# Sink-window attention woven with a cosine FFN: q and k of the third half loaded in 32-row groups and turned by VectorE, and four tiles for the sinks' rows of v

## The chip, the cores and the metric

The kernel runs on one core of one Trainium2 chip. The time is device microseconds, the median of three runs. The engines are TensorE (PE in the profile; its weight loads are PEld), VectorE (DVE), ScalarE (ACT), GpSimd (POOL) and SyncE (SP), which issues the transfers of this case.

## The reference

Three layers follow each other. Attention has 4 batches, 8 heads, 768 positions and head dimension 64; a position sees the 4 sinks and the 128 positions that end with itself. Its output, 3072 tokens by 512, goes through an FFN with a cosine, and that through a mixture of 8 experts, of which each token takes one.

```python
scores = scale * np.matmul(q, k.transpose(0, 1, 3, 2))
keep = is_sink | in_window
a = softmax(np.where(keep, scores, -1e9))
x = np.matmul(a, v)              # to 3072 x 512
h = x @ w_in                     # 512 -> 2048
x = (h * np.cos(h)) @ w_out      # 2048 -> 512
logits = x @ w_gate + modality_bias[modality_id]
e = argmax(logits)
out = softmax(logits)[e] * (relu(x @ w1[e]) @ w2[e])
```

## The kernel before

**Halves and pairs.** Attention is cut into eight halves, `hb` 0 to 7: a half is 384 positions (three blocks of 128) of one batch, for all eight heads. Heads are taken two at a time, so a half has four pairs (`pr` 0 to 3), with one head in partitions 0 to 63 and the other in 64 to 127. The third half, which the change touches, is `hb = 2`: the first 384 positions of the second batch, with three blocks of keys. It runs from about 113 to 204 us in the trace. For each pair, `attn_front` loads q and k (and starts v), brings them to the form [head dimension, position] in `qT` and `kT`, and hands on to `mid` (scores `ps`, row maxima, exponentials into `Pb`) and `rest` (division, transposes `pt`, product with v in `po`).

**Two ways to turn q and k.** Up to the third half (`hb < STACK = 3`) lines 442 and 443 load 128 positions on the partitions, in runs of 64 numbers; TensorE transposes block by block into a PSUM bank (`pq` at L466, `pk` at L480, three blocks each in the third half), and ScalarE copies the bank to `qT` (L472) and `kT` (L494). From the fourth half on, lines 437 and 439 load four groups of 32 partitions, one for each half of each head's dimension, in runs of 32 numbers, so that VectorE's transposes of 32x32 blocks (L462, L476) give the wanted form by themselves. There the operands are also split in a high and a low part (`q_r` to two tiles `qT`, `k_r` to two tiles `kT`), by ScalarE (L469, L489) and VectorE (L149).

**The sinks' rows of v.** Line 451 loads the sinks' rows of v of a pair into one of two tiles, `vs_n0` and `vs_n1`, by `pr % 2`. From the fourth half on, GpSimd makes the operand `vs_r` of them (L609, L610, L149).

**The FFN.** `ffn_tile_gen` goes over 384 tokens at a time, in 16 chunks of 128 hidden columns. A chunk has 12 matmuls into a bank `hp` (two such banks); VectorE (L143, L146), ScalarE (L738) and VectorE (L149) make `ch` = h cos h of it and free the bank; ScalarE and GpSimd split it into `g_h` and `g_l` (L748, L149); and 9 matmuls `y` (L676) multiply it by the high and low part of w_out. The low part, `wo_l`, is read back from memory for each chunk (L721, three buffers). Beside the first halves a converter makes all high and low weights: loads `cv_in` and `cv_out`, chains on VectorE and ScalarE (`cv_a`, `wi_l`, `wo_l`, L301, L141, L146), and stores of `wo_l` (L304). Its last step lies at about 204 us, where the fourth half begins.

**What sets the order.** The code is written with generators that `weave` and `merge` advance by weights, and a scheduler in the framework orders the instructions of each engine. What runs is a fixed order for each engine. SP issues these transfers one after the other, and one that waits for a buffer holds up those behind it.

## Time and profile before

| | us |
|---|---|
| median of three runs | 1129.12 |
| lowest and highest | 1128.71 and 1129.29 |
| profiled execution | 1130.26 |
| its span, first to last instruction | 1128.5 |
| TensorE busy in the span | 1085.8 (96%) |
| VectorE busy in the span | 700.3 (62%) |
| mean granted clock of TensorE | 0.993 |

The span is what the views show; 1.76 us of the profiled execution lie outside it. Matmuls are pipelined, so a matmul's own duration is longer than the distance to the start of the next one; that distance is what it costs TensorE.

### The profile page before, as it was taken

The page shows a single profiled execution, that of the slowest core. Times are in us where ns is not written, and L with a number is a line of the kernel's source. Part 1 is how long each engine was busy: PE and PEld are TensorE (multiplying, and loading weights), DVE is VectorE, ACT ScalarE, POOL GpSimd, SP SyncE. Part 2 cuts the span into 40 slices and gives each one's busy share as a digit, 9 for nine tenths or more (in the row PEclk, how much of TensorE's full clock was granted, in tenths as well). Part 3 has the DMA queues.
Part 4 walks back from the last instruction along what each step waited for, and adds up shares of the span by engine and source line. Part 5 has one row for each costly group of instructions (what it writes and reads, how often), then busy time and mean ns, then how long its engine had stood idle before and what let it go on. Part 6 is the DMA issues. An engine that isn't in the chain of part 4 may idle for free.

```text
span 1128.5 us, 20688 instructions
## 1 busy us (share of the span) xinstructions
PE 1085.8 (96%) x6432; PEld 917.2 (81%) x6432; DVE 700.3 (62%) x2186; ACT 607.9 (54%) x1243; POOL 247.3 (22%) x337
## 2 busy tenths in 40 slices
PE   5989999999999999999999999999999998999995
PEld 3667777788788888888888889899889997899984
DVE  6677888777977877886787674746731225522210
ACT  4879888665676666665766553334222225422221
POOL 1232233322212221222222211321112211221110
PEclk9989999999999999999999999999999999999998
DMA  6466675433332542433342132624151115111110
GB/s 152 134 187 181 199 232 147 102 83 83 89 91 68 111 89 65 101 75 82 74 107 68 56 114 73 254 64 114 47 188 58 58 40 188 39 59 40 40 41 24
DMA packets 171155, 113.38 MB, mean 100 GB/s; under 512 B 130799, under 2 KB 138991, under 8 KB 170992
## 3 DMA queue, kind: packets, MB, share of 16 engines
q1 hardware_dynamic: 166672, 97.88, 32.3%
q0 software_dynamic: 4320, 13.65, 3.7%
q8 instruction: 63, 1.03, 0.4%
q14 instruction: 100, 0.82, 0.2%
HBM read 151.06 MB, written 19.67 MB: 151 GB/s over the span
## 4 chain that ended last, share of the span: by engine, by line
PE 82%; DVE 6%; DMA 4%; ACT 3%; issue 2%; POOL 1%; SPq 0%; DVEq 0%; ACTq 0%; POOLq 0%
PE hp L137 21%; PE y L676 20%; PE m_y L137 11%; PE m_h L137 10%; PE ps L137 5%; PE po L137 5%; DMA out_dram<-m_ot,m_ids 3%; PE pl L804 1%; PE pt L589 1%; PE mh L137 1%; PE yT L793 1%; PE m_a L1143 1%; DMA cv_in<-in_moe_w_in_dram 1%; PE pt L588 1%; PE pz L626 1%
## 5 line engine op out<-in xcount | busy, mean ns | idle before, releaser
L149 POOL TENSOR_TENSOR g_l<-ch,g_h 128x384 fp32r<-128x384 f32 x128 | 133.6, 1044 | 471.6 <-ACT g_h L748 408.6
L137 PE MATMUL hp<-xT_h,wi_h 128*128 128x384 f32 x512 | 186.4, 364 | 2.2 <-DVE ch L149 2.2
L137 PE MATMUL hp<-xT_h,wi_l 128*128 128x384 f32 x512 | 175.1, 342 | 0.0
L137 PE MATMUL hp<-xT_l,wi_h 128*128 128x384 f32 x512 | 174.5, 341 | 0.0
L676 PE MATMUL y<-wo_l,g_h 128*128 128x512 f32 x384 | 155.7, 406 | 2.2 <-DMA wo_l<-wl_scr 2.2
L676 PE MATMUL y<-wo,g_h 128*128 128x512 f32 x384 | 156.9, 410 | 0.0
L676 PE MATMUL y<-wo,g_l 128*128 128x512 f32 x384 | 154.5, 402 | 0.2 <-POOL g_l L149 0.2
L738 ACT ACTIVATE ch<-ch,cols 128x384 f32<-128x384 f32 x128 | 78.7, 616 | 107.8 <-DVE ch L146 107.1
L137 PE MATMUL m_y<-wi_h,hT 128*128 128x512 f32 x416 | 132.5, 393 | 0.7 <-issue 0.5
L146 DVE SCALAR_TENSOR_TENSOR hT<-m_h,hT 128x256 fp32r<-128x256 f32 x88 | 37.4, 424 | 151.0 <-ACTq L1337 102.3
L137 PEld LDWEIGHTS hp<-xT_h,wi_h 128*128 128x128 f32 x512 | 96.9, 189 | 15.5 <-issue 4.5
L748 ACT ACTIVATE g_h<-ch 128x384 fp32r<-128x384 f32 x128 | 66.3, 520 | 69.7 <-DVE ch L149 46.2
L137 PEld LDWEIGHTS hp<-xT_l,wi_h 128*128 128x128 f32 x512 | 97.2, 190 | 4.4 <-issue 1.0
L143 DVE TENSOR_SCALAR ch<-hp 128x384 int32<-128x384 f32 x128 | 70.8, 553 | 46.6 <-PE hp L137 35.4
L137 PEld LDWEIGHTS hp<-xT_h,wi_l 128*128 128x128 f32 x512 | 96.8, 189 | 1.7 <-issue 1.4
L137 PEld LDWEIGHTS m_y<-wi_h,hT 128*128 128x128 f32 x416 | 78.1, 188 | 17.0 <-issue 0.9
L149 DVE TENSOR_TENSOR ch<-ch,hp 128x384 f32<-128x384 f32 x128 | 70.0, 547 | 29.7 <-ACT ch L738 29.2
L551 ACT ACTIVATE Pb<-Pb,mx 128x272 f32<-128x272 f32 (+1 forms) x168 | 82.8, 494 | 8.4 <-DVE mx L534 7.5
L676 PEld LDWEIGHTS y<-wo,g_l 128*128 128x128 f32 x384 | 72.3, 188 | 15.1 <-POOL g_l L149 1.0
L676 PEld LDWEIGHTS y<-wo,g_h 128*128 128x128 f32 x384 | 72.3, 188 | 13.9 <-issue 3.6
L676 PEld LDWEIGHTS y<-wo_l,g_h 128*128 128x128 f32 x384 | 72.5, 189 | 11.3 <-DMA wo_l<-wl_scr 2.5
L1154 ACT ACTIVATE hT<-m_h 128x256 fp32r<-128x256 f32 x88 | 34.0, 387 | 87.6 <-PE m_h L137 86.6
(289 smaller groups left out, 2288.8 us busy)
## 6 DMA issues: line engine op xcount, KB each, us to landing
rw<-in_moe_w_dram SPq DMA_DIRECT2D x112, 512.0 KB
wo_l<-wl_scr SPq DMA_DIRECT2D x122, 256.0 KB
cv_in<-in_moe_w_in_dram SPq DMA_DIRECT2D x16, 512.0 KB
cv_out<-in_moe_w_out_dram SPq DMA_DIRECT2D x16, 512.0 KB
y_scr<-yt SPq DMA_DIRECT2D x24, 256.5 KB
xT_h<-xg_h SPq DMA_DIRECT2D x32, 192.0 KB
xT_l<-xg_l SPq DMA_DIRECT2D x32, 192.0 KB
wl_scr<-wo_l SPq DMA_DIRECT2D x16, 256.0 KB
```

Source lines behind the costliest of these rows:

```text
L137: PE.matmul(o, l, r, start=start, stop=stop)
L143: e.tensor_scalar(out=o, in0=i, scalar1=s1, scalar2=s2, op0=op0, op1=op1)
L146: e.scalar_tensor_tensor(out=o, in0=i0, scalar=s, in1=i1, op0=op0, op1=op1)
L149: e.tensor_tensor(out=o, in0=a, in1=b, op=op)
L551: ACT.activation(out=Pb[t][j][:, c0:c1], in_=Pb[t][j][:, c0:c1], func=AF.Exp, scale=-1.0, bias=mx[:, i:i + 1], accum_out=sm[:, i:i + 1])
L588: PE.transpose(pt[:, j, 0:P], Pb[t][j][:, 0:P], ident)
L589: PE.transpose(pt[:, j, P:2 * P], Pb[t][j][:, SEG:W3], ident)
L626: PE.transpose(pz[0:nr, t * P:(t + 1) * P], pi_, ident)
L676: i = PE.matmul(o, l, r, start=start, stop=stop)
L738: ACT.activation(out=ch, in_=ch, func=AF.Sin, scale=TWO_PI, bias=half_pi)
L748: ACT.activation(out=gh, in_=ch, func=AF.Copy)
L1154: ACT.activation(out=hT_h[f], in_=hp, func=AF.Relu)
```

## The change

For `hb = 2` the four pairs load q and k as the later halves do, in four groups of 32 partitions, and VectorE's transposes write `qT[0]` and `kT[0]` directly: this half is not split in high and low parts, so no `q_r` or `k_r` is needed. Twenty-four transposes on TensorE (12 `pq`, 12 `pk`) and eight copies on ScalarE (four at L472, four at L494) are no longer there; eight transposes on VectorE and sixteen more loads are. The eight PSUM banks of `pq` and `pk` are no longer taken. The small copies of the sinks' keys (L486, L496) read `kT[0]` in place of the bank.

From the fourth half on, the sinks' rows of v go to a tile for each pair: two more tiles, in the memory that the converter has given back, cleared once by GpSimd.

```diff
--- before.py
+++ after.py
@@ -413,7 +413,11 @@
                 sp2[i] = apool.tile([P, HALF], F32R, name=f"sp_r{i}", tag=f"sp{i}")
                 POOL.memset(vsr2[i].bitcast(F32), 0.0)
                 POOL.memset(sp2[i].bitcast(F32), 0.0)
-        vs_n, sp = vs_n2[pr % 2], sp2[pr % 2]
+        if stacked and len(vs_n2) < NPAIR:
+            for i in range(2, NPAIR):
+                vs_n2.append(late_pool().tile([P, 2 * D], F32, name=f"vs_n{i}"))
+                POOL.memset(vs_n2[i][0:2 * NS], 0.0)
+        vs_n, sp = vs_n2[pr if stacked else pr % 2], sp2[pr % 2]
         n_ps = [0]
 
         def psb(name):
@@ -429,7 +433,7 @@
             qn = apool.tile([P, NQ, 2, D], F32, name="qn")
             kn = apool.tile([P, 4, 2, D], F32, name="kn")
             vn = None
-        turned = hb >= STACK
+        turned = hb >= 2
         qf, kf_ = [t.rearrange("p t j d -> p (t j d)") for t in (qn, kn)] if turned else (None, None)
         for j in range(4 if turned else 2):
             if turned:
@@ -472,13 +476,19 @@
             ACT.activation(out=qT[0], in_=pq[:, 0:HALF], func=AF.Copy)
         yield steps(hb)[0]
         if turned:
-            pk = late_pool().tile([P, 4 * P], F32, name="k_r")
-            DVE.transpose(out=pk[:, 0:nblk * P], in_=kf_[:, 0:nblk * P])
+            if stack:
+                pk = late_pool().tile([P, 4 * P], F32, name="k_r")
+                pk3 = pk.rearrange("p (t s) -> p t s", s=P)
+            else:
+                pk3 = kT[0]
+            DVE.transpose(out=pk3[:, 0:nblk, 0:P].rearrange("p t (c i) -> p t c i", i=TB),
+                          in_=kf_[:, 0:nblk * P].rearrange("p (t c d) -> p t c d", c=4, d=TB))
         else:
             pk = psb("pk")
         for t in range(0 if turned else nblk):
             PE.transpose(pk[:, t * P:(t + 1) * P], kn[:, t].rearrange("p j d -> p (j d)"), ident)
-        pk3 = pk.rearrange("p (t s) -> p t s", s=P)
+        if not turned:
+            pk3 = pk.rearrange("p (t s) -> p t s", s=P)
         if half == 0:
             if hb + 1 < STACK:
                 DVE.tensor_copy(ks[:, pr, 0], pk3[:, 0, 0:NS])
@@ -491,7 +501,8 @@
             for i in range(2):
                 DVE.tensor_copy(kT[i][:, 0:nblk - 1, P:SEG], ks[:, pr, i:i + 1, :].to_broadcast([P, nblk - 1, NS]))
         else:
-            ACT.activation(out=kT[0][:, 0:nblk, 0:P], in_=pk3[:, 0:nblk, :], func=AF.Copy)
+            if not turned:
+                ACT.activation(out=kT[0][:, 0:nblk, 0:P], in_=pk3[:, 0:nblk, :], func=AF.Copy)
             src = pk3[:, 0:1, 0:NS] if half == 0 else ks[:, pr, 0:1, :]
             DVE.tensor_copy(kT[0][:, 0:nblk - 1, P:SEG], src.to_broadcast([P, nblk - 1, NS]))
         yield steps(hb)[0]
```

Lines of the changed kernel are numbered 4 higher behind the first piece and 11 higher behind the third: L462 is L466 there, L476 is L484, L676 is L687, L721 is L732.

On TensorE at the first pair of the third half, there stands before (`pq` and `pk` are the transposes, `hp` a chunk of the next FFN tile, `y` the second product):

```order
L676 MATMUL y2_1413<-wo3_113,g_l_1551 128x512
L466 MATMUL pq_1787<-ident_70,qn_1774 128x128 x3
L137 MATMUL hp_1792<-xT_h_1115,wi_h0_78 128x384
...
L137 MATMUL hp_1792<-xT_h_1115,wi_l0_88 128x384
L480 MATMUL pk_1799<-ident_70,kn_1775 128x128 x3
L137 MATMUL hp_1792<-xT_h_1115,wi_h0_78 128x384
...
L676 MATMUL y1_1412<-wo4_114,g_h_1662 128x512
L137 MATMUL ps_1813<-kT_1786,qT_1785 128x128
```

On VectorE at the same place, there stands now (`wi_l8` is a step of the converter, `ks` the sinks' keys):

```order
L149 TENSOR_TENSOR wi_l8_96<-cv_a_1746,wi_h8_86 128x512
L466 STREAM_TRANSPOSE qT_1789<-qn_1774 128x384
L484 STREAM_TRANSPOSE kT_1790<-kn_1775 128x3x128
L141 TENSOR_SCALAR cv_a_1826<-cv_h_1824 128x512
L496 CAST ks_135<-kT_1790 128x16
L507 COPY kT_1790<-kT_1790 128x2x16
L545 ISA Pb_1806,mx_1807<-ps_1809,masks_200 128x128
```

The transposes have moved from TensorE, among its matmuls, to VectorE, behind the converter's step and ahead of the row maxima of the scores.

On VectorE at the start of the fourth half, there stands before (`wo_l_2749` is the converter's last step, `hp_2849` and `hp_2895` the last two chunks of an FFN tile):

```order
L149 TENSOR_TENSOR wo_l_2749<-cv_a_2715,wo15_125 128x512
L462 STREAM_TRANSPOSE q_r_2760<-qn_2730 128x384
L476 STREAM_TRANSPOSE k_r_2767<-kn_2731 128x512
L143 TENSOR_SCALAR ch_2871<-hp_2849 128x384
L149 TENSOR_TENSOR qT_2746<-q_r_2760,qT_2745 128x384
L149 TENSOR_TENSOR kT_2748<-k_r_2767,kT_2747 128x4x128
...
L143 TENSOR_SCALAR ch_2908<-hp_2895 128x384
```

and now (`wo_l_2714` is the same step, `hp_2883` the last chunk of that tile):

```order
L149 TENSOR_TENSOR wo_l_2714<-cv_a_2699,wo15_125 128x512
L143 TENSOR_SCALAR ch_2896<-hp_2883 128x384
L146 SCALAR_TENSOR_TENSOR ch_2896<-hp_2883,ch_2896 128x384
L149 TENSOR_TENSOR ch_2896<-ch_2896,hp_2883 128x384
L466 STREAM_TRANSPOSE q_r_2748<-qn_2729 128x384
L149 TENSOR_TENSOR qT_2745<-q_r_2748,qT_2744 128x384
L484 STREAM_TRANSPOSE k_r_2755<-kn_2730 128x512
L502 CAST kT_2747<-ks_135 128x3x16
L149 TENSOR_TENSOR kT_2747<-k_r_2755,kT_2746 128x4x128
L545 ISA Pb_2918,mx_2919<-ps_2921,masks_200 128x272
```

The transposes of the fourth half's first pair stood ahead of the last two chunks' `ch`; now they stand behind the last chunk's. On TensorE the 12 matmuls of `hp_2883` are now followed by 18 of the next tile (9 for each bank) and then by the scores `ps_2921`.

On SP at the start of the fourth half, there stands before:

```order
L450 DMA vn_2740<-in_v_dram 128x4x64
L451 DMA vs_n0_136<-in_v_dram 16x64
L450 DMA vn_2740<-in_v_dram 128x4x64
L451 DMA vs_n0_136<-in_v_dram 16x64 x3
L451 DMA vs_n1_137<-in_v_dram 16x64 x2
L721 DMA wo_l_2781<-wl_scr_59 128x512
L304 DMA wl_scr_59<-wo_l_2749 128x512
L721 DMA wo_l_2847<-wl_scr_59 128x512
```

and now:

```order
L304 DMA wl_scr_59<-wo_l_2714 128x512
...
L454 DMA vn_2739<-in_v_dram 128x4x64
L455 DMA vs_n0_136<-in_v_dram 16x64
L454 DMA vn_2739<-in_v_dram 128x4x64
L455 DMA vs_n0_136<-in_v_dram 16x64
L732 DMA wo_l_2769<-wl_scr_59 128x512
L732 DMA wo_l_2835<-wl_scr_59 128x512
```

The sinks' rows of the later pairs no longer stand between the first pair's and `wo_l`; the converter's last store now stands ahead of that `wo_l`, and seven transfers between them. On TensorE, three `y` matmuls of the high part are followed by 30 of `hp` and 8 of `ps` before the first one that reads `wo_l_2769`; before, five of `hp` lay between them and the first that reads `wo_l_2781`.

## Rows read from the trace of the kernel before

**Rows 1.** The page, busy time and share of the span of each engine.

```profile
PE 1085.8 (96%) x6432; PEld 917.2 (81%) x6432; DVE 700.3 (62%) x2186; ACT 607.9 (54%) x1243; POOL 247.3 (22%) x337
```

**Rows 2.** Busy by stage: length; PE, PEld, DVE, ACT, POOL; clock, DMA share, GB/s.

```profile
113.00:178.00 65.00, 62.96 (x333) 47.67 (x332) 56.95 (x154) 54.91 (x112) 20.80 (x32) 1.00 0.67 201
...
204.00:212.00 8.00, 5.79 (x30) 4.93 (x29) 4.88 (x11) 2.31 (x5) 2.98 (x5) 1.00 0.50 152
```

**Rows 3.** Waits of PE, 113 to 212 us: us in total, times, longest.

```profile
PE y L676 <- DMA wo_l<-wl_scr: 2.2, 1, 2.2
PE pt L589 <- POOL Pb L143: 1.5, 2, 0.8
```

**Rows 4.** PE by time around pair 1: start, length, operation, idle before it.

```profile
124.65 0.40 PE L676 MATMUL y<-wo,g_l 128*128 128x512 f32 x1
124.88 0.49 PE L466 MATMUL pq<-ident,qn 128*128 128x128 f32 x3
125.12 0.48 PE L676 MATMUL y<-wo,g_h 128*128 128x512 f32 x1
125.44 0.39 PE L676 MATMUL y<-wo_l,g_h 128*128 128x512 f32 x1
...
129.05 0.68 PE L589 MATMUL pt<-ident,Pb 128*128 128x128 f32 x2 [0.72 <-POOL Pb L143]
```

**Rows 5.** Line 466 in the third half: count, ns min/median/max.

```profile
L466 PE MATMUL pq<-ident,qn x12: 270/272/273, 114.0 to 172.5; 128*128 128x128 f32 x12
```

**Rows 6.** DVE by line and shape, whole span: count, busy us, mean ns.

```profile
L149 DVE TENSOR_TENSOR ch<-ch,hp 128x384 f32<-128x384 f32 x128 | 70.0, 547 | 29.7 <-ACT ch L738 29.2
...
L462 DVE STREAM_TRANSPOSE q_r<-qn 128x384 f32<-128x384 f32 x20 | 11.4, 569 | 1.8 <-DMA qn<-in_q_dram 1.8
L149 DVE TENSOR_TENSOR qT<-q_r,qT 128x384 fp32r<-128x384 f32 x20 | 11.0, 549 | 0.0
...
L149 DVE TENSOR_TENSOR kT<-k_r,kT 128x512 fp32r<-128x512 f32 x12 | 8.1, 679 | 0.0
```

**Rows 7.** ACT by line and shape, whole span.

```profile
L738 ACT ACTIVATE ch<-ch,cols 128x384 f32<-128x384 f32 x128 | 78.7, 616 | 107.8 <-DVE ch L146 107.1
...
L469 ACT ACTIVATE qT<-q_r 128x384 fp32r<-128x384 f32 x20 | 10.3, 517 | 6.0 <-PE ps L137 5.1 <-DVE q_r L462 0.8
...
L489 ACT ACTIVATE kT<-k_r 128x512 fp32r<-128x512 f32 x12 | 7.4, 619 | 1.1 <-DVE k_r L476 1.1
```

**Rows 8.** DVE by time at the start of the fourth half.

```profile
203.19 0.87 DVE L149 TENSOR_TENSOR wo_l<-cv_a,wo 128x512 fp32r<-128x512 f32 x1 [0.23 <-ACT wo L301]
204.10 0.58 DVE L462 STREAM_TRANSPOSE q_r<-qn 128x384 f32<-128x384 f32 x1
204.60 0.67 DVE L476 STREAM_TRANSPOSE k_r<-kn 128x512 f32<-128x512 f32 x1
205.19 0.52 DVE L143 TENSOR_SCALAR ch<-hp 128x384 int32<-128x384 f32 x1
```

**Rows 9.** PE by time at the start of the fourth half.

```profile
205.27 0.33 PE L137 MATMUL hp<-xT_h,wi_h 128*128 128x384 f32 x1
205.44 0.34 PE L137 MATMUL hp<-xT_l,wi_h 128*128 128x384 f32 x1
...
208.52 0.50 PE L676 MATMUL y<-wo_l,g_h 128*128 128x512 f32 x1 [2.21 <-DMA wo_l<-wl_scr]
```

**Rows 10.** SP by time at the start of the fourth half.

```profile
197.61 7.64 SPq L451 DMA_DIRECT2D vs_n<-in_v_dram  x5
205.30 0.41 SPq L721 DMA_DIRECT2D wo_l<-wl_scr  x1
```

**Rows 11.** DVE by time at pair 0 of the third half.

```profile
115.04 1.16 DVE L149 TENSOR_TENSOR wi_l<-cv_a,wi_h 128x512 fp32r<-128x512 f32 x1
```

**Rows 12.** PE by time at pair 0 of the third half.

```profile
116.93 0.39 PE L676 MATMUL y<-wo,g_h 128*128 128x512 f32 x1
117.37 1.01 PE L137 MATMUL ps<-kT,qT 64*128 64x128 f32 x6
```

## The prediction

> **What bounds the kernel now.** I read the shares of the engines first: TensorE is busy for 1085.8 of the 1128.5 us of the span, VectorE for 700.3 [rows 1]. So a saving counts where it shortens TensorE's queue or a wait of it. Then the busy time by stage [rows 2]. In the stretch of the third half, 113 to 178 us, TensorE is busy for 62.96 of 65 us, at full granted clock (1.00, the 2.4 GHz level). VectorE stands at 56.95 and ScalarE at 54.91 there, far above their share of the whole span, since the converter runs beside it: this is the place where VectorE has least to give. In the 8 us from 204, where the fourth half begins, TensorE is busy for only 5.79. The waits tell why [rows 3]: between 113 and 212 us TensorE waits once, 2.2 us, for a `wo_l` from memory, and twice, 1.5 us together, for GpSimd's division of `Pb`. So the third half is bounded by TensorE's own queue, with VectorE close behind, and its end has one hole of 2.2 us that is a late transfer.
>
> **Twenty-four transposes leave TensorE.** A record of one is 272 ns long [rows 5], but matmuls overlap, so the distance between starts is the cost. In rows 4, `y` follows `y` after 0.23 us (124.65 to 124.88). From the first of the three `pq` (124.88) to the second `y` behind them (125.44) it is 0.56, and 0.23 of it is the `y` at 125.12. So three transposes cost 0.56 - 0.23 = 0.33 us, one 0.11. The half has 12 of `pq` [rows 5] and, by the code, as many of `pk`: 24 x 0.11 = 2.65 us (eight groups of 0.33) that come off the queue. The bounds are 0 (other waits swallow it) and 24 x 0.272 = 6.5 (every record at its full length, which rows 4 refute); I take 2.65.
>
> The Trainium skill, "TensorE: Matmul & The Clock Gate", Part 4 (PE-mode transpose), puts a 128x128 transpose at about 275 ns within a kernel. The trace agrees for the length of the record, 272 ns, but not as a price among matmuls, 110 ns; by the page the term would be 24 x 0.275 = 6.6 and the time about 1123.3 (an estimate), and by the measured distance it is 2.65.
>
> **Eight copies leave ScalarE, eight transposes come to VectorE.** ScalarE is bound at neither place; its gain I take as nothing. On VectorE a transpose of 128x384 costs 0.50 us from start to start (204.10 to 204.60), one of 128x512 0.59 [rows 8]. All eight have 384 columns: 8 x 0.50 = 4.0 us. VectorE's cover for them is the idle time of the stretch, 65 - 56.95 = 8.05 us, which shrinks to 65 - 2.65 - 60.95 = 1.4 if TensorE delivers all its saving there. The bounds on the path are 0 and 4.0. At pairs 1 to 3 I take 0, since fronts are issued ahead of need (the second pair's `pq`, 124.88, stands 4.2 us ahead of the first pair's `pt`, 129.05 [rows 4]). At pair 0 there is no such room. Before, the scores `ps` start at 117.37, behind the fourth `y` at 116.93 [rows 12], which would have let them start at 116.93 + 0.23 = 117.16. Without two groups of transposes (-0.66) and with two more `y` ahead of `ps` in the new order (+0.46) TensorE comes there at 116.96. VectorE has the converter's `wi_l` until 115.04 + 1.16 = 116.20 [rows 11], then two transposes, 1.0 us and some 0.1 to hand over: 117.3. So TensorE waits 0.3 to 0.4; I take +0.4, with bounds 0 and 1.0 (both transposes).
>
> **What may swallow the saving.** The two waits for GpSimd, 0.72 at 129.05 [rows 4] and the other of the same total of 1.5 [rows 3], lie in this half: if the chain that ends in `Pb` does not start earlier, TensorE arrives earlier and waits longer. In the order, TensorE's matmuls of the FFN are moved ahead in such places, so I leave the term at 2.65 and put the loss in the range (up to 1.3, four groups of 0.33).
>
> **The hole of 2.21 us at the start of the fourth half.** Before, SP spends 7.64 us on five sinks' loads in a row [rows 10], among them those of two later pairs, which wait until GpSimd has read the two tiles. The `wo_l` behind them is issued at 205.30 and TensorE gets on at 208.52 [rows 9, 10], 3.2 us later. Four tiles take these loads out of that row, and they come with their own pair. In return the new order has the converter's last store ahead of that `wo_l`; its data is ready at 203.19 + 0.87 = 204.06 [rows 8], and the store and seven issues follow: 8 x 0.41 = 3.3, so 207.4, and 210.6 with landing. That would be later than before. But TensorE now has 30 `hp` and 8 `ps` between the last `y` of the high part and the first that needs this tile, where there were five `hp`; at 0.17 us each (205.27 to 205.44, [rows 9]) that is 38 x 0.17 = 6.5 us against the 0.9 of before. The wait has 5.6 us more cover and comes 2.1 later: it goes. Term: -2.21, bounds -2.21 and +1.
>
> **A new wait at the same place.** VectorE's transposes of the fourth half's first pair stand behind the last chunk's `ch` now. So a chain starts when TensorE ends `hp_2883`: L143, L146, ScalarE's sine, L149, `q_r`, ScalarE's `qT`, VectorE's `qT`, `k_r`, ScalarE's `kT`, then the scores. With 0.55 for L143 and L146 too (the same shape as L149's 547 ns) and the lengths of [rows 6, 7] and 0.67 for `k_r` (its length in [rows 8]): 0.55 + 0.55 + 0.62 + 0.55 + 0.57 + 0.52 + 0.55 + 0.67 + 0.62 = 5.2, and 0.5 for the hand-overs between engines, an estimate: about twice the 0.23 us that VectorE stands idle for ScalarE ahead of 203.19 [rows 8]. That is 5.7. TensorE's cover is 18 `hp` of the next tile, 18 x 0.17 = 3.1 (nine of them wait for the bank that L149 frees, within that chain). VectorE's low part of `kT` (0.68) stands behind, and the scores on it come fourth: +0.3. So 5.7 - 3.1 + 0.3 = +2.9. The bounds are 0 (these durations are lengths, and what starts behind one starts up to 0.1 sooner; the order of the matmuls may also let VectorE be ahead) and +4.
>
> **The rest** goes together at nothing: GpSimd's two clearings of 32 rows lie on an engine that is busy for 20.80 of 65 us [rows 2], the eight banks that are no longer taken can only let others start sooner, and the sinks' copies read the same few numbers. SP has 16 more issues of about 0.41, 6.6 us in the third half; that is the fourth rival.
>
> **Sum.** -2.65 + 0.4 - 2.21 + 2.9 = -1.6, to which I add -0.2 for the 0.2 us that TensorE already waits at pair 0 before (117.16 to 117.37) and that the +0.4 replaces: -1.8. On the profiled execution the span goes from 1128.5 to 1126.7, and with the 1.76 outside it 1130.26 becomes 1128.5. That execution lies 1.14 above the median, so the median goes from 1129.12 to **1127.3**. A measurement of this kernel tells 0.2% from no change, 2.26 us: below 1126.86 is faster, above 1131.38 slower. So the likeliest case lies at the edge of "within".
>
> **The rivals.**
>
> *Both holes close* (1124.4). The new chain at the fourth half is covered: the scheduler placed it by its own count, and rows 8 show these steps starting 0.45 to 0.59 apart rather than at their lengths. Then -2.65 - 2.21 + 0.4 - 0.2 = -4.7, and up to 1.5 more if the waits for GpSimd go too: 1122.9 to 1125.5, and I take 1124.4. For it speaks that after 212 us this kernel's TensorE is never held long by such chains; against it the count of 18 matmuls.
>
> *VectorE becomes the bound* (1131.9), the case on the other side. Its place is the third half: two transposes per pair in a queue that has 8.05 us left in 65. If none finds idle time, 4.0 us come on the path of the `ch` steps and of the row maxima, and TensorE waits for the bank that L149 frees. -1.8 + 4.0 + 0.6 (eight hand-overs at 0.07, an estimate) = +2.8. It makes the kernel slower than before once 1.8 of the 4.0 us, four of the eight transposes, are on the path. For it speaks 56.95 of 65; against it that the waits of rows 3 name no VectorE. The Trainium skill, "VectorE: DVE Perf Modes", Rules for kernel authors, would leave 128x128 transposes on TensorE where the result may go to PSUM, and gives VectorE the 32x32 ones: the first half of that rule speaks for this rival; no run here shows it yet.
>
> *The loads come late* (1129.1). q and k come in runs of 32 numbers instead of 64, twice the packets, from twice the issues, while DMA is busy for 0.67 of the stretch [rows 2]. If SP's 6.6 us delay a converter's load or a `wo_l` by 1.8 us where TensorE needs it, the gain is gone. That the later halves live with the same loads speaks against it, but their DMA has no converter beside it.
>
> *The change doesn't do what it says* can't be: the order shows the transposes gone and the loads spread.
>
> **How the numbers follow.** The forecast has 0.43 (its own range 1125.7 to 1129.4, of it 0.16 below 1126.86 and 0.27 within), both holes closed 0.27 (all faster; within it 0.02 that transposes are worth their whole records, 1123.4 by [rows 5]), VectorE the bound 0.19 (0.14 slower, 0.05 within), late loads 0.11 (0.07 within, 0.04 slower). Faster 0.43, within 0.39, slower 0.18. From 1123.0 to 1131.6 lies all but about 0.06 below and 0.12 above.
>
> **What would show it.** In the changed kernel's waits of TensorE there should be no 2.2 us for `wo_l` near 208 us, and one or two waits of together some 2.5 us at about 208 to 212 us at the first scores of the fourth half or at `hp` for the bank. In the third half TensorE's busy time should fall by about 2.7 us, VectorE's rise by about 4, and the half should end 2 us earlier. A third half as long as before, or waits of `hp` for VectorE's L149 in it, show the second rival; waits of `y` for `wo_l` or of the converter for `cv_in` the third. The forecast is wrong if a stretch behind 300 us changes its length by over 1 us, since nothing here touches it.

## The result: 1.05% slower, and the profile after

The changed kernel takes 1139.93 us (median of six runs, 1137.77 to 1141.76) against 1128.11 of the kernel before: a ratio of 1.0105, 95% interval 1.0090 to 1.0121. The forecast was 1127.3 with a range up to 1131.6. It was wrong in sign, and the time lies outside the range. The profiled execution of after is the shortest of its six (1137.77, span 1136.0); that of before was above its median, so the two traces show 7.5 us of the 11.8.

The page and the stretches of [rows 1, 2], now for the changed kernel (length; PE, PEld, DVE, ACT, POOL; clock, DMA share, GB/s):

```profile
PE 1085.7 (96%) x6408; PEld 916.7 (81%) x6408; DVE 708.5 (62%) x2194; ACT 605.7 (53%) x1235; POOL 251.5 (22%) x339
```

```profile
113.00:178.00 65.00, 59.23 (x286) 45.24 (x285) 55.03 (x142) 47.48 (x91) 20.08 (x28) 0.92 0.54 163
178.00:204.00 26.00, 22.78 (x122) 17.77 (x121) 23.58 (x58) 17.80 (x40) 8.02 (x11) 1.00 0.65 187
204.00:212.00 8.00, 7.02 (x44) 5.16 (x44) 7.73 (x16) 5.68 (x10) 4.75 (x8) 1.00 0.27 62
```

TensorE's busy time in the span is the same as before to 0.1 us, though 24 transposes are gone. The stretch from 113 to 178 us had 62.96 us busy at a clock of 1.00; now it has 59.23 at 0.92. Every engine is less busy there: this is a stretch of waits, not of an overloaded engine.

The work has shifted in time, so stretches at fixed times compare badly. Landmarks do better: the last `po` of the second half (it reads `ld_x`) and the last product of `sp` and `vs_n` in the third. The same view between these two, first of before and then of after:

```profile
110.80:202.10 91.30, 89.17 (x480) 68.46 (x476) 80.15 (x209) 75.35 (x152) 30.11 (x45) 1.00 0.62 183
```

```profile
108.70:210.70 102.00, 92.03 (x461) 71.08 (x458) 89.43 (x219) 73.39 (x145) 32.48 (x44) 0.95 0.55 162
```

The third half is 10.7 us longer. From there to the last `hp` it is 587.9 us before (202.1 to 790.0) and 587.3 after (210.7 to 798.0). So the whole loss lies in the third half. (That it begins 2.1 us earlier is scatter: with the sinks' tiles alone, below, it begins at 108.7 too.) The 10.7 us are made of four pieces. TensorE's idle time rose from 91.30 - 89.17 = 2.13 to 9.97, +7.84. The mean clock of 0.95 takes 0.05 x 102 = 5.10, of which some 4.6 are a cost (below). What is left of the busy time at full clock is 92.03 - 4.6 = 87.4. Some 0.9 of it is work that only moved here: the matmuls between the landmarks fall by 19 (480 to 461) and not by 24, so about five more of the next tile's `hp`, at 0.17 us each [rows 9], lie between them. The remainder, 86.5 against 89.17, is -2.6, near the -2.65 that the 24 transposes were priced at; as a remainder it is an estimate. Together +10.7.

TensorE's waits of after, 100 to 215 us, where [rows 3] had two lines (us in total, times, longest):

```profile
PE pt L599 <- POOL Pb L143: 3.7, 3, 1.4
PE pt L600 <- POOL Pb L143: 1.7, 3, 0.8
PE hp L137 <- DVE ch L149: 1.7, 1, 1.7
PE pt L590 <- ACT pT L602: 1.4, 1, 1.4
PE pt L590 <- POOL Pb L143: 0.5, 1, 0.5
PE ps L137 <- DVE kT L507: 0.4, 1, 0.4
PE po L137 <- ACT sp L638: 0.4, 1, 0.4
PE ps L137 <- DVE kT L484: 0.2, 1, 0.2
```

The wait for `wo_l` is gone. The transposes of the second pair to the fourth aren't named at all: nobody waits long for `qT` or `kT`. TensorE waits most for GpSimd's division of `Pb`, at the other end of each pair's softmax: 3.7 + 1.7 + 0.5 = 5.9 us, where it was 1.5.

Why that division is late is read from GpSimd's and VectorE's rows at the second pair. GpSimd before, then GpSimd after, then VectorE after (start, length, operation, idle before it):

```profile
152.09 2.62 POOL L143 TENSOR_SCALAR Pb<-Pb,sm 128x128 f32<-128x128 f32 x6
```

```profile
148.32 0.72 POOL L143 TENSOR_SCALAR Pb<-Pb,sm 128x128 f32<-128x128 f32 x2 [15.11 <-ACT y_part L777]
149.71 1.01 POOL L149 TENSOR_TENSOR g_l<-ch,g_h 128x384 fp32r<-128x384 f32 x1 [0.67 <-PE y L687]
151.18 0.91 POOL L143 TENSOR_SCALAR Pb<-Pb,sm 128x272 f32<-128x272 f32 x1 [0.46 <-DVE sm L569]
152.06 0.99 POOL L149 TENSOR_TENSOR g_l<-ch,g_h 128x384 fp32r<-128x384 f32 x1
153.04 0.93 POOL L143 TENSOR_SCALAR Pb<-Pb,sm 128x272 f32<-128x272 f32 x1
156.25 1.18 POOL L143 TENSOR_SCALAR Pb<-Pb,sm 128x144 f32<-128x144 f32 x2 [2.29 <-ACT ch L749]
```

```profile
147.96 0.17 DVE L569 RECIPROCAL sm<-sm 128x2 f32<-128x2 f32 x1
149.03 0.69 DVE L149 TENSOR_TENSOR wo_l<-cv_a,wo 128x512 fp32r<-128x512 f32 x1 [0.90 <-PE y L687]
149.64 0.16 DVE L141 TENSOR_SCALAR sm<-sm 128x2 f32<-128x2 f32 x1
149.76 1.25 DVE L141 TENSOR_SCALAR cv_a<-cv_h 128x512 int32<-128x512 int32 x1
150.93 0.15 DVE L569 RECIPROCAL sm<-sm 128x2 f32<-128x2 f32 x1
```

Before, six divisions run in a row, 2.62 us. After, they stand in four pieces over 9.1 us (148.32 to 157.43), with GpSimd's and VectorE's other work between them, the converter's `wo_l` and `cv_a` among it. And the waits have a price of their own. TensorE by time at this place, and the stretches of 4 us around it:

```profile
149.06 0.40 PE L687 MATMUL y<-wo,g_h 128*128 128x512 f32 x1
149.29 0.39 PE L687 MATMUL y<-wo_l,g_h 128*128 128x512 f32 x1
...
152.15 0.33 PE L599 MATMUL pt<-ident,Pb 128*128 128x128 f32 x1 [1.31 <-POOL Pb L143]
...
154.02 0.48 PE L599 MATMUL pt<-ident,Pb 128*128 128x128 f32 x1 [1.43 <-POOL Pb L143]
...
157.07 0.63 PE L687 MATMUL y<-wo,g_h 128*128 128x512 f32 x1
157.49 0.63 PE L687 MATMUL y<-wo_l,g_h 128*128 128x512 f32 x1
```

```profile
128.00:132.00 4.00, 2.26 (x12) 1.72 (x13) 3.26 (x7) 2.44 (x7) 1.24 (x4) 1.00 0.33 73
132.00:136.00 4.00, 4.00 (x22) 2.64 (x22) 4.00 (x7) 1.54 (x3) 1.22 (x1) 0.57 0.00 0
...
148.00:152.00 4.00, 2.84 (x14) 1.96 (x12) 3.10 (x7) 3.91 (x13) 2.56 (x4) 1.00 0.70 208
152.00:156.00 4.00, 2.42 (x8) 1.90 (x9) 4.00 (x9) 2.42 (x4) 1.96 (x3) 0.63 0.62 198
156.00:160.00 4.00, 4.00 (x11) 3.10 (x11) 4.00 (x9) 2.87 (x6) 2.75 (x4) 0.52 0.70 198
```

The same `y` follow each other after 0.23 us at 149 and after 0.42 at 157: the granted clock is at its lower level, 1.2 GHz, for most of 132 to 136 and 152 to 160. Ahead of the first fall TensorE was busy for 2.26 of 4 us; ahead of the second for 2.84 of 4, with most of a wait of 1.31 us among them. These three stretches lose 1.72 + 1.48 + 1.92 = 5.1 us of clock, all of the third half's share. The second fall lies near 153.0 (1.48 us lost up to 156 are 2.96 us at half speed), and TensorE stands idle until 154.02, so about 1.0 us at the lower level costs nothing: the price is some 4.6 us. Before, the clock is 1.00 throughout the third half.

The last difference is on SP. q and k have one buffer each. Before, the four loads of the third pair are issued from 125.4 to 127.9 and those of the fourth from 148.2 to 152.3; after, the eight of the third pair from 145.6 to 159.8 and those of the fourth from 179.3 to 188.7. The first and the last of the third pair's `qn` and `kn` loads, before and after:

```profile
125.40 0.38 SPq L442 DMA_DIRECT2D qn<-in_q_dram  x1
...
127.92 0.50 SPq L443 DMA_DIRECT2D kn<-in_k_dram  x1
```

```profile
145.60 0.50 SPq L441 DMA_DIRECT2D qn<-in_q_dram  x1
...
159.79 0.47 SPq L443 DMA_DIRECT2D kn<-in_k_dram  x1
```

The turns are late too: TensorE began them at 114.0, 124.9, 147.5 and 172.3; VectorE does at 114.0, 135.1, 167.3 and 194.1. Before, SP went to the next loads right behind a turn (125.4 behind 124.9, 148.2 behind 147.5). In the changed kernel the second pair is turned by 136.7, and SP comes to the next loads at 145.6. It waits at none of the loads of q and k for the buffer (L441 and L443 are not among its waits); they stand in its order behind stores that wait for other engines. Its two longest waits, 105 to 212 us:

```profile
SPq L304 <- DVE wo_l L149: 15.4, 3, 9.6
SPq L778 <- ACT y_part L777: 13.8, 3, 9.4
```

Nor does VectorE stand idle for a load ahead of any turn of this kernel. So here the turns and the loads are late by their places in the queues.

### The profile page after: what moved, and what is told of

Its sections match the earlier page's. It is cut to its first block, busy times and chain, and to the rows that moved or that the text cites. A ratio compares the mean times of both kernels' runs of the same rounds, so it can differ in the third digit from the quotient of the medians.

```text
span 1136.0 us, 20622 instructions
## 1 busy us (share of the span) xinstructions
PE 1085.7 (96%) x6408; PEld 916.7 (81%) x6408; DVE 708.5 (62%) x2194; ACT 605.7 (53%) x1235; POOL 251.5 (22%) x339
## 3 DMA queue, kind: packets, MB, share of 16 engines
q8 instruction: 64, 1.05, 0.4%
## 4 chain that ended last, share of the span: by engine, by line
PE 81%; DVE 7%; DMA 4%; ACT 3%; issue 2%; POOL 1%; SPq 1%; DVEq 0%; POOLq 0%; ACTq 0%
PE hp L137 22%; PE y L687 22%; PE m_h L137 10%; PE m_y L137 9%; PE ps L137 5%; PE po L137 5%; DMA out_dram<-m_ot,m_ids 3%; PE pl L815 1%; PE yT L804 1%; PE mh L137 1%; PE pt L600 1%; PE m_a L1154 1%; PE pt L590 1%; PE pz L637 1%; POOL Pb L143 1%
## 5 line engine op out<-in xcount | busy, mean ns | idle before, releaser
L687 PE MATMUL y<-wo_l,g_h 128*128 128x512 f32 x384 | 156.6, 408 | 0.0
L687 PE MATMUL y<-wo,g_l 128*128 128x512 f32 x384 | 155.6, 405 | 0.2 <-POOL g_l L149 0.2
L687 PE MATMUL y<-wo,g_h 128*128 128x512 f32 x384 | 155.1, 410 | 0.0
L687 PEld LDWEIGHTS y<-wo,g_l 128*128 128x128 f32 x384 | 73.0, 190 | 14.6 <-POOL g_l L149 1.0
L687 PEld LDWEIGHTS y<-wo,g_h 128*128 128x128 f32 x384 | 72.5, 189 | 13.7 <-issue 2.8
L137 PE MATMUL ps<-kT,qT 64*128 64x272 f32 (+1 forms) x504 | 72.5, 353 | 10.0 <-ACT kT L505 6.4
L137 PE MATMUL m_y<-wi_l,hT 128*128 128x512 f32 x208 | 81.0, 390 | 0.0
```

Of the source, the lines that this page charges most:

```text
L137: PE.matmul(o, l, r, start=start, stop=stop)
L687: i = PE.matmul(o, l, r, start=start, stop=stop)
```

## The experiments

First theory: VectorE's added work delays the softmax (the second rival). Rivals: the new order of the queues; the split loads; the sinks' tiles. "Order kept" below means that the order of an engine's instructions in the third half is that of another kernel, forced by dependencies that carry order alone; instructions that the other kernel doesn't have (VectorE's eight transposes above all) are in no such list and find their place by themselves:

```diff
+    for k_, runs_ in ORDERS.items():
+        seq_ = [kept[k_][s_ + n_] for s_, c_ in runs_ for n_ in range(c_)]
+        for x_, y_ in zip(seq_, seq_[1:]):
+            tc.add_manual_dep(y_, x_.name, edge, reason="kept")
```

All results, each with the ratio to the kernel before on the same chip, and from its trace the length of the third half between the two landmarks, TensorE's idle time in it and its mean clock. The last three columns are of one profiled execution; that of turned_sp_kept (1136.42 us) is the longest of its twelve, 4 us above their median, so its row looks worse than the kernel is.

| kernel | ratio [95%] | third half | idle | clock |
|---|---|---|---|---|
| before | 1 | 91.3 | 2.13 | 1.00 |
| after | 1.0105 [1.0090, 1.0121] | 102.0 | 9.97 | 0.95 |
| part1_turned | 1.0091 [1.0070, 1.0111] | 104.4 | 10.27 | 0.93 |
| part2_four_tiles | 0.9996 [0.9984, 1.0008] | 91.3 | 2.13 | 1.00 |
| before_with_after_order | 1.0029 [1.0017, 1.0041] | 97.7 | 5.75 | 0.98 |
| after_with_before_order | 1.0149 [1.0130, 1.0167] | 108.7 | 15.66 | 0.94 |
| before_split_loads | 0.9995 [0.9983, 1.0007] | 92.0 | 2.65 | 1.00 |
| before_more_vectore | 1.0024 [1.0009, 1.0040] | 93.8 | 3.97 | 1.00 |
| turned_all_orders_kept | 1.0067 [1.0047, 1.0087] | 103.3 | 11.93 | 0.95 |
| turned_sp_kept | 1.0026 [1.0014, 1.0037] | 96.0 | 5.12 | 0.96 |
| turned_sp_kept_two_buffers | 1.0028 [1.0016, 1.0039] | 95.0 | 5.62 | 0.98 |
| turned_behind_softmax | 1.0060 [1.0044, 1.0077] | 101.7 | 10.35 | 0.97 |
| turned_sp_kept_behind_softmax | 1.0085 [1.0067, 1.0103] | 102.4 | 11.27 | 0.95 |
| turned_two_buffers | 1.0028 [1.0012, 1.0043] | 95.0 | 5.83 | 0.98 |
| turned_two_buffers_early_k | 1.0034 [1.0021, 1.0047] | 95.6 | 6.24 | 0.98 |
| copied_not_turned | 1.0151 [1.0131, 1.0172] | 101.2 | 10.75 | 0.95 |
| copied_order_kept | 1.0102 [1.0083, 1.0121] | 106.5 | 13.71 | 0.94 |
| copied_sp_kept | 1.0104 [1.0086, 1.0121] | 108.9 | 13.49 | 0.92 |

### Which part, and is it TensorE's order

part1_turned is the change without the two more tiles for the sinks' rows:

```diff
-        turned = hb >= STACK
+        turned = hb >= 2
...
```

> The third half's q and k turned by VectorE, with two tiles for the sinks' rows of v as before. The changed kernel came out at about 1140 us beside 1128; TensorE's clock is at 1.2 GHz for about 10 us of its third half. If the first part alone is the cause (both by the order it gives TensorE and by VectorE's load): 1137 to 1142, with the low clock between 130 and 160 us. If the four tiles of v are the cause, within 1 us of 1126.5 (the 2.65 us of transposes come off, or nothing).

part2_four_tiles has these two tiles alone:

```diff
...
-        vs_n, sp = vs_n2[pr % 2], sp2[pr % 2]
+        vs_n, sp = vs_n2[pr if stacked else pr % 2], sp2[pr % 2]
```

> Four tiles for the sinks' rows of v from the fourth half on, the third half as before. TensorE's order differs from before in a few places of the fourth half alone. If the first part is the cause of the loss: 1126 to 1129, the wait for wo_l at 208 us (2.2 us) gone and up to 2.2 us gained. If the second part is the cause: over 1135.

The loss comes with the turning alone. The four tiles alone change nothing, and they don't even close the hole that they were credited with; TensorE's wait at the start of the fourth half in part2_four_tiles (compare the first line of [rows 3]):

```profile
PE y L680 <- DMA wo_l<-wl_scr: 1.8, 1, 1.8
```

Next, the two programs with each other's order of TensorE: after_with_before_order is the program of after, before_with_after_order that of before. All other engines are free. The edit is the same in both, with another list:

```diff
...
+    keep = [pe_ins[s + n] for s, c in PE_ORDER for n in range(c)]
+    for x, y in zip(keep, keep[1:]):
+        tc.add_manual_dep(y, x.name, edge, reason="kept")
```

> The changed kernel, its transposes on VectorE, but TensorE's matmuls of the third half and of the start of the fourth in the order in which the kernel before has them (without the 24 transposes). Theory 'order': the loss is the new order of TensorE's queue, in which the FFN's matmuls stand ahead of the places where TensorE waits for the softmax; then this gives 1124 to 1129, no low clock after 130 us, and waits for Pb of no more than 2 us in the third half. Theory 'VectorE': its 4 us of transposes are on the path whatever the order; then 1135 to 1141. Theory 'loads': q and k come late in the short runs; then as the second, with waits of the turned q for its load.

> The kernel before, its transposes on TensorE, but TensorE's other matmuls of the third half and of the start of the fourth in the order of the changed kernel. Theory 'order': 1136 to 1142 (the loss of 11 us, the 24 transposes filling up to 2.65 us of the waits), with waits for Pb and a low clock as in the changed kernel. Theory 'VectorE' or 'loads': within 2 us of 1128.

TensorE's order is not the cause by itself: with the order of before the program of after is slower still (1.0149), and the order of after costs the program of before 1.0029 only, under a third of the loss. The orders of the other queues have to fit it.

### Packets and VectorE's work, each by itself

before_split_loads is the kernel before, its order kept, with q and k of the third half in runs of 32 numbers:

```diff
+            for d_ in ((slice(0, TB), slice(TB, D)) if hb == 2 else (slice(0, D),)):
+                SP.dma_start(out=qn[:, :, j, d_], in_=q[b, h0 + j, half * HALF:(half + 1) * HALF, d_].rearrange("(t p) d -> p t d", p=P))
...
```

> The kernel before, with each load of q and k of the third half in two of 32 columns: twice the packets and sixteen more issues on SP, the data and TensorE's transposes as before, the order of four engines kept. Theory 'loads': 1132 or more. The others: within 1.5 us of 1128.5.

before_more_vectore is the kernel before, its order kept, with eight more transposes on VectorE that nobody reads; that of q is shown, that of k is like it:

```diff
+            if hb == 2:
+                DVE.transpose(out=apool.tile([P, HALF], F32, name="xs"), in_=qn.rearrange("p t j d -> p (t j d)"))
```

> The kernel before, with eight transposes of 128x384 more on VectorE in the third half, whose result nobody reads; TensorE's transposes stay and the order of four engines is kept. They add 4 us to VectorE and nothing to TensorE. Theory 'VectorE': 1131 to 1134 (each transpose on the path of the steps behind it), more waits of TensorE for L149 or Pb. The others: within 1.5 us of 1128.5.

Sixteen more loads and twice the packets cost nothing (0.9995), and neither does keeping four engines' order by force, which this run does too. The Trainium skill, "DMA: Bandwidth & Descriptors", Why small descriptors are slow, names a fixed overhead per packet that weighs on small ones; where the transfers have slack, as here, this run shows nothing of it.

Eight more transposes on VectorE cost 1.0024, 2.7 us, where they were forecast to cost 0 and the rival had them at 4.6. They read the loads as well, so SP waits for them too, 1.5 us in all. They show as a later `Pb`, from 1.5 us in [rows 3] to 2.5:

```profile
PE pt L118 <- POOL Pb L118: 2.5, 3, 1.6
```

(In the kernels with a kept order every line is that of a helper; operations go by their tiles.)

### All orders kept, and SP's apart

turned_all_orders_kept is the program of part1_turned with the order of before on TensorE, VectorE, ScalarE and GpSimd; SP is free. turned_sp_kept has before's order on SP too, each load of q and k in two. First against part1_turned, then the second against the first:

```diff
...
+    PE, ACT, DVE, POOL = [Kept(e_, k_) for e_, k_ in ((PE, "PE"), (ACT, "ACT"), (DVE, "DVE"), (POOL, "POOL"))]
```

> The first part of the change alone, with the third half and the start of the fourth in the order of the kernel before on TensorE, VectorE, ScalarE and GpSimd; the eight transposes stand on VectorE just ahead of the copies of the sinks' keys. SP's order is free. The run that kept TensorE's order alone was 17 us slower, with VectorE's and ScalarE's queues in another order than TensorE's, so it told nothing of VectorE's load. Theory 'joint order' (the loss is how the scheduler sets the queues of all engines anew): 1124 to 1129, no low clock in the third half. Theory 'VectorE' (4 us of transposes on the path in a stretch where it is busy for 88%): 1133 to 1141. Theory 'loads': as the second, with waits of the transposes or of the converter for loads.

```diff
-    PE, ACT, DVE, POOL = [Kept(e_, k_) for e_, k_ in ((PE, "PE"), (ACT, "ACT"), (DVE, "DVE"), (POOL, "POOL"))]
+    PE, ACT, DVE, POOL, SP = [Kept(e_, k_) for e_, k_ in ((PE, "PE"), (ACT, "ACT"), (DVE, "DVE"), (POOL, "POOL"), (SP, "SP"))]
```

> As the run with the orders of four engines kept (8 us slower), with SP's transfers of the third half in the order of the kernel before too (the order that was harmless with split loads). It differs from that run in SP's order alone. Theory 'SP order' (q and k, and the converter's loads, stand behind waiting transfers in the new order of SP): 1127 to 1131. Theory 'one buffer' (q and k of the next pair wait until VectorE has turned this pair's, and SP's queue stands meanwhile): 1134 or more, with SP waiting for the transposes.

With four orders kept the loss is 1.0067, which its interval doesn't part from the 1.0091 of part1_turned. VectorE and then TensorE by time at the third pair's turn show what is left:

```profile
158.31 0.58 DVE L118 STREAM_TRANSPOSE qT<-qn 128x384 f32<-128x384 f32 x1 [2.45 <-DMA cv_out<-in_moe_w_out_dram]
...
160.53 0.22 DVE L118 RECIPROCAL sm<-sm 128x2 f32<-128x2 f32 x2
```

```profile
161.51 1.76 PE L118 MATMUL pt<-ident,Pb 128*128 128x128 f32 x5 [5.03 <-POOL Pb L118]
```

VectorE stands 2.45 us before the transpose, for a transfer (the profile names the converter's; the last loads of this pair's q and k were issued at 153.29 and 153.79, against 126.86 and 127.92 before). Behind it in the queue are the reciprocals of the pair ahead, behind those GpSimd's division, and TensorE waits 5.03 us. TensorE's turn of before, at 147.5, held nobody's softmax. With SP's order kept too, the same pair's loads are issued by 132.1, VectorE turns it at 138.2 and 141.5, and the ratio falls to 1.0026; the two intervals don't touch. The order in which SP issues the loads, with the place of the turns that goes with it, is worth 0.4%, some 5 us. From part1_turned to turned_sp_kept, with all five queues in the order of before, the loss falls from 0.91% to 0.26%, and the intervals lie far apart: seven tenths of it are the new orders, since VectorE does the turns in both.

### Where VectorE turns, and who frees the buffer

Here the later pairs' transposes are in VectorE's list, behind the softmax steps of the pair ahead, so that a late load can't hold those. turned_behind_softmax is without SP's order, turned_sp_kept_behind_softmax with it, and turned_two_buffers has a second buffer of q and k besides, for every other pair. The first edit is shown by VectorE's order at the third pair's turn, the second is the one of turned_sp_kept. In the first, steps in between are left out.

```diff
-STREAM_TRANSPOSE qT<-qn
-STREAM_TRANSPOSE kT<-kn
 RECIPROCAL sm<-sm
 TENSOR_TENSOR Pb<-Pb
 RECIPROCAL sm<-sm
+STREAM_TRANSPOSE qT<-qn
+STREAM_TRANSPOSE kT<-kn
```

> The first part of the change in the order of the kernel before on four engines, as in the run that came out 8 us slower; but each later pair's two transposes, and the small copies of the sinks' keys with them, stand on VectorE behind the softmax steps of the pair before (pairs 1 and 2: behind its pT; pair 3: behind its last reciprocal) and no longer ahead of them. In the earlier run VectorE's sums sm stood behind the transposes, and GpSimd's Pb and TensorE's pt waited for them (3.1, 5.0 and 1.1 us). Theory 'place on VectorE': those waits fall below 1 us each and the time is 1126 to 1131. Theory 'load of VectorE whatever the place', or loads that come late: 1134 or more.

> As turned_sp_kept, with the later pairs' transposes behind the softmax steps of the pair before. SP order and place together: 1125 to 1129 if these two are all that is wrong. If q's and k's single buffer holds SP, slower than turned_sp_kept, since the buffer comes free later.

```diff
+        elif hb == 2 and pr % 2:
+            qn = qk2[0].tile([P, NQ, 2, D], F32, name="qn")
+            kn = qk2[0].tile([P, 3, 2, D], F32, name="kn")
...
```

> As turned_sp_kept_behind_softmax, with a second buffer for q and k of the odd pairs of the third half, so that a load no longer waits for VectorE's transposes of the pair before. Theory 'one buffer': 1124 to 1128 here while turned_sp_kept_behind_softmax is over 1130. Otherwise the two are equal within 1.5 us.

SP's order, which had brought 0.4%, brings nothing at this place of the turns (1.0060, then 1.0085). The longest waits of SP, ScalarE and TensorE in turned_sp_kept_behind_softmax tell why:

```profile
SPq L118 <- DVE qT L118: 22.7, 3, 8.6
```

```profile
137.63 0.60 ACT L118 ACTIVATE y_part<-y 128x512 f32<-128x512 f32 x1 [6.32 <-DMA yp_scr<-y_part]
138.28 0.80 PE L118 MATMUL y<-wo,g_h 128*128 128x512 f32 x1 [5.41 <-ACT y_part L118]
```

SP stands 22.7 us at loads of q that wait until VectorE has read the one buffer. Everything behind them is late, so the stores of `y_part`: ScalarE waits 6.32 us for one of them before it can fill the tile again, and TensorE 5.41 for ScalarE. With the second buffer the line is gone and the ratio is 1.0028; the intervals don't touch.

Two more runs ask what is left. At the first pair TensorE waits 1.63 us for the sinks' keys in `kT`, a small copy on VectorE; turned_two_buffers_early_k has it up close behind the transpose (the expectation puts this copy on ScalarE by mistake), and the pair's transposes in the list, where they come at 114.3 instead of before 108. turned_sp_kept_two_buffers gives turned_sp_kept the second buffer of turned_two_buffers, by the same edit. The first in VectorE's order:

```diff
 CAST ks<-kT
+COPY kT<-kT
-TENSOR_SCALAR cv_a<-cv_h
 TENSOR_TENSOR ks<-kT,ks
+TENSOR_SCALAR cv_a<-cv_h
 SCALAR_TENSOR_TENSOR cv_a<-cv_h,cv_a
-COPY kT<-kT
```

> The kernel of turned_two_buffers (q and k turned by VectorE, a second buffer of each for every other pair, SP's loads in the order of the kernel before, the later pairs' turns behind the softmax of the pair ahead), with ScalarE's copy of k for the group's first pair directly behind its turn. If the first pair's hole is what is left, the third half shortens by 1 to 2 us and the ratio falls to 1.001 to 1.002; if VectorE's load and the low clock behind the other waits are what is left, it stays at 1.002 to 1.004.

> The kernel of turned_sp_kept (all orders of the kernel before but ScalarE's copies of k, SP's too, the turns on VectorE at the place where TensorE made them) with a second buffer of q and k for every other pair. If the single buffer costs anything while the turns stand early, SP's loads come free sooner and the ratio falls below the 1.0026 of turned_sp_kept; if the buffer only mattered because the turns stood late behind the softmax, it stays at 1.002 to 1.003.

Neither moves the time (1.0034 and 1.0028). The wait of 1.63 us at the first pair only became three of 0.62, 0.54 and 0.91. And the second buffer is worth nothing where VectorE turns early (1.0026 without it): the single buffer costs where the turn stands late in VectorE's queue and SP's order has the next load early. In the changed kernel, whose own order has those loads late, SP waits for it nowhere.

### Nobody turns

These leave the third half's transposes out, so its attention isn't the reference's: ScalarE copies q and k as they are. copied_not_turned has the order that comes by itself, copied_order_kept that of before on TensorE, VectorE and GpSimd, copied_sp_kept SP's too; their edits to the order are as above. The copy of q is shown, that of k is like it:

```diff
-            DVE.transpose(out=pq, in_=qf)
+            if hb == 2:
+                ACT.activation(out=pq, in_=qf, func=AF.Copy)
```

> The first part of the change with the scheduler's own order, but q and k of the third half are copied by ScalarE (eight copies, as many as before) and not turned by anything: the transposes of this half are left out, on TensorE and on VectorE. Theory 'VectorE' (its transposes and their place in its queue make the loss): 1124 to 1129. Theory 'scheduler' (with the fronts off TensorE, the queues are set anew and worse, whatever turns q and k): 1134 to 1142.

> The same without any transposes in the third half (left out; ScalarE copies q and k), with TensorE, VectorE and GpSimd in the order of the kernel before; ScalarE's order is free. It shows what 24 transposes off TensorE are worth where nothing else moves. If they are worth their distance between starts, 1125 to 1127 (2.65 us less, part of it lost in waits for Pb); if their time is slack, 1128 to 1129; if ScalarE's other order costs, over 1130 with waits for ScalarE.

> No transposes in the third half (left out; ScalarE copies q and k), with TensorE, VectorE, GpSimd and SP in the order of the kernel before and ScalarE's order free; it was 12 us slower with SP's order free. Theory 'SP order': 1125 to 1131. If it stays over 1136, neither VectorE's transposes nor SP's order is the cause there, and ScalarE's order is next.

With nothing more on VectorE (79.37 us busy in the third half of copied_order_kept, 80.15 before) the loss is as large (1.0102). So a loss of this size needs no added work on VectorE; how much of the changed kernel's is VectorE's work these three don't tell. (Of copied_not_turned's 17 us, some 6 lie behind the third half: 594.2 us to the last `hp` where it was 587.9.) ScalarE's queue now does what VectorE's did; VectorE's longest wait in copied_order_kept:

```profile
DVE ks L118 <- ACT kT L118: 8.8, 4, 3.2
```

ScalarE's order was free in these, since the order of before can't be had with one buffer: SP's load of the next q would wait for a copy that stands behind a step which needs a load behind that q. So copied_sp_kept says nothing on SP's order by itself. That its third half is the longest of all stays unexplained in detail.

## Why the prediction was wrong

**Right.** The 24 transposes left TensorE's work: -2.65 forecast, -2.6 as the remainder of the third half's rows. At pair 0 TensorE waits 0.4 + 0.2 us for `kT`, +0.4 forecast. The wait for `wo_l` went, though not by the four tiles that it was credited to: with them alone 1.8 us stay, and in part1_turned, without them, the wait is gone. That term came right by another way, the new order of the queues. The new chain at the start of the fourth half is there, 2.17 us where 2.9 were forecast, in the two places named:

```profile
217.69 0.44 PE L137 MATMUL hp<-xT_h,wi_h 128*128 128x384 f32 x1 [1.04 <-DVE ch L149]
220.67 0.51 PE L137 MATMUL ps<-kT,qT 64*128 64x272 f32 x3 [1.13 <-ACT kT L499]
```

Behind the third half no stretch changed (587.9 and 587.3 us).

**The steps that failed: "At pairs 1 to 3 I take 0, since fronts are issued ahead of need", and the "up to 1.3" for the waits for GpSimd.** The zero asked whether the transposes' results would be late, and they aren't. The 1.3 asked whether TensorE would come earlier to divisions of `Pb` that stay where they were. Neither asked what the new orders do to the steps that end in `Pb`. These came late: the waits for `Pb` went from 1.5 to 5.9 us, the third half's idle time rose by 7.84 in all, and the clock took some 4.6 more. Even the slowest rival stood at 1131.9 us. Before, the divisions of the second pair stood in a row; now the softmax's small steps stand between the converter's on VectorE. The runs show that the orders make most of this: with those of before on all five queues the loss falls from 0.91% to 0.26%. The steps that moved weren't in the diff, and my reading of the new order covered the first pair and the fourth half alone: the turns of the second to fourth pair, 10, 20 and 22 us later than before, and the loads of the third pair, 20 to 32 us later, could not be seen there.

**Late loads were looked for in the wrong place.** The rival of late loads was priced at 1.8 us for SP's own 6.6 us of issue. These cost nothing (before_split_loads). What costs is the order in which SP issues, some 5 us between turned_all_orders_kept and turned_sp_kept; and, with that order, the buffer: 6.4 us (1.0085 to 1.0028) between one and two where the turns stand late. What SP's order alone is worth amid the changed kernel's other orders was not tried.

**VectorE's cover.** 8.05 us of idle time were set against 4.0 us of transposes, and the term was 0. By itself that load costs 2.7, though VectorE is busy for only 82.98 of the 93.8 us of the third half in before_more_vectore: idle time elsewhere in a queue that runs in order did not cover it. The Trainium skill, "VectorE: DVE Perf Modes", Rules for kernel authors, leaves a 128x128 transpose on TensorE where the result may go to PSUM; the runs agree: with the queues' orders of before, and with a second buffer or without, the turn on VectorE is still 0.26 to 0.28% slower than TensorE's.

**No term for the clock.** Behind the waits the granted clock fell twice, and some 4.6 of the 10.7 us are that. "What may swallow the saving" had up to 1.3 us in all. A small reading was off too: the 0.2 us taken off as a wait at pair 0 is none of TensorE's waits in the trace; the one of 0.2 us stands at 119.02.

**What stays open.** Of the last 0.26% (2.9 us) about 2.7 is what VectorE's added work cost in before_more_vectore, but then the 2.65 us that left TensorE should show as a gain, and they don't. In the traces of these kernels the idle time (5.1 to 5.8) and a clock of 0.96 to 0.98 take it; of turned_sp_kept's 3.0 us more idle time 1.6 are the wait for `kT` at the first pair and 1.4 more waits for `Pb`. before_more_vectore has 3.97 us idle at a clock of 1.00. Why its waits leave the clock alone and these don't wasn't settled. Nor was it tried why the order that came by itself puts the loads so late. No kernel here beats the one before.

## What to carry to other kernels

When an operation moves to another engine, list what it frees (the buffer it reads, and the transfer that waits for that buffer) and what stands behind it in the new queue, not only its time and who reads its result. A queue that runs in order and waits for a load holds up everything behind it (2.45 us on VectorE became 5.03 on TensorE), and a single buffer hands that wait on to the queue that issues the transfers (22.7 us on SP). In a kernel woven by a scheduler, compare the start of each moved step in both orders along the whole stretch, not at its ends; and where the busiest engine stood at full clock with hardly a wait, allow for a lower clock behind new waits.

## What the runs showed of the hardware

Waits can cost more than their length: in after 7.84 us more idle time came with some 4.6 us lost at the 1.2 GHz level. The clock fell first behind waits of 0.73 and 1.71 us (they end at 126.73 and 131.01), and again behind one of 1.31 and within the next, of 1.43 (they end at 152.15 and 154.02). A wait need not do it: after's own of 1.41 us at 183.75 left the clock at 1.00 (the stretch from 178 to 204), and before, from 152 to 156 us, TensorE waits once, 0.80 us, is busy for 3.05 of 4 us, and the clock stays:

```profile
152.00:156.00 4.00, 3.05 (x17) 2.40 (x18) 1.37 (x6) 3.17 (x5) 2.92 (x8) 1.00 0.92 260
156.00:160.00 4.00, 4.00 (x29) 2.79 (x28) 4.00 (x8) 2.85 (x7) 1.11 (x1) 1.00 0.33 100
```

A VectorE step of one shape (`cv_a<-cv_h`, 128x512) takes 0.42 us at 130.88 and 1.25 at 149.76, where GpSimd's `g_l` runs beside it from 149.71 to 150.72. That is no single case: in after this step takes 0.41 to 0.43 us all 23 times that no GpSimd step runs beside it, and 1.22, 1.25, 1.23 and 1.15 where it begins while a `g_l` is running (at 132.28, 149.76, 158.17 and 202.53); before, 1.23 the one time (142.07). So a new order also changes how long steps take. What that is worth here no run tells.
